# Attention over a window with an MLP over tokens behind it, in one kernel: tail evictions freed of the other bank of a PSUM pair, and the order written anew

## The chip, the cores and the metric

The kernel runs on one core of a Trainium2 chip. The metric is the time of the program on the device in microseconds (us). TensorE is called PE (its loads of weights PEld), VectorE DVE, ScalarE ACT, GpSimd POOL and SyncE SP.

## The reference

```python
# q, k, v: (8 batches, 8 heads, 576 positions, 64), float32
scores = (q @ k.T) / 8
bias = slopes[h] * -abs(i - j)                 # slopes 2**-(h+1)
mask = (i - j >= 0) & (i - j < 128)
attn = softmax(where(mask, scores + bias, -1e9))
x = (attn @ v) put together over heads         # (8, 576, 512)
wq, wk = x @ w_q, x @ w_k                      # (8, 576, 64) each
W_tok = wq @ wk.T / 8                          # (8, 576, 576)
out = maximum(W_tok @ x, 0) @ w_out            # (8, 576, 512), float32
```

## The kernel before

A batch has four blocks of 128 positions and a tail of 64. The kernel takes the batches in turn, and two batches at a time in the MLP. Each step is an operation with a short name; the number behind it is the batch (for the MLP the first batch of the two), then a part. In order of the data:

- **Loads.** `LF` (first batch, by SP and ACT queues), `Lq`, `Lk`, `Lv`, `Lt` (tails of q and k) on POOL's queue, which also converts to 16 bits; `Lw` and `Lwo` load the weights on SP's queue, and wait for `wz`, a tiny memset on DVE.
- **Set-up.** `ident` (POOL) and `idh` (its 16-bit copy, DVE), `iota` and `mask` (POOL) with `wmc` (DVE) between them, `bias` (ACT, 8 exponentials of the distances), `ones` (DVE: in each of the four buffers of v a memset of the unused half of the tail and one of a column of ones, whose product gives the sums), `zeros`, `pads`, `warm`; `WM` are matmuls on nothing that keep PE busy.
- **Transposes of q and k** on PE: `TF`, `TJ` (first batch), `TQ`, `TK`, `TT` (tails), and their evictions from PSUM `EF`, `EJ`, `ETQ`, `ETK`, `ETT`.
- **Attention.** `QK` b.g.u is the scores of block g and half u of the heads, `EXP` the exponential on ACT (L660), `MUL` the product with the bias on DVE (L669), `PV` b.t the product with v for query block t; t = 4 is the tail, which takes one bank instead of two. On DVE follow `RC`, the reciprocal of the sums (L723, for the tail L720 into `invt`), and `X`, the product that evicts (L733, for the tail L727 into `xtl`).
- **MLP.** `XT`, `XTT` transpose x, `EXT`, `EXTT` evict; `WQ`, `WK`, `WT` (tail) are the projections, `EWQ`, `EWK`, `EWT` their evictions; `G` is wk.T @ x and `EG` its eviction; `MX` the mixing, `RM`, `RMT` the relu that evicts it (`RM` one of the pair's two banks each); `OUT` the output product, `EO` its eviction, `DO` the store on SP's queue. `CWQ` and `CW` convert the weights.

PSUM is four tiles `pair0` to `pair3` of two banks each. Most products take a pair, the others one bank of a pair.

The order is written out by hand in the string `ORDER`: a word such as `QK0.2.1:P2` or `RC0.4:D` names the operation and its place (D, A, G, S: the engine; P2: pair 2, both banks; P21: pair 2, bank 1). `follow` reads it and each engine runs its operations in that order. Waits between engines come from the tiles that are read and written. As a pair is one tile, two operations in its two banks would wait for each other; `apart` declares such instructions free of order. It takes the instructions that an operation has handed to `hold`, puts them into a group of their bank and engine, and frees them of the other bank's groups of the other engines, other than true dependencies (`keep`). An operation finds its bank by its own PSUM (`banks`) or by what it frees (`frees`). `RC` and `X` hand nothing to `hold`.

The order of the first operations around the change is: on POOL `Lq0.2`, `iota`, `ident`, `Lk0.2`, `Lk0.1`, `Lk0.3`, `mask`, `Lq1.0`; on DVE `warm`, `ones`, `pads`, `idh`, `wmc`; on ACT `EF0.1.1`, `bias`, `EXP0.0.1`, `EXP0.2.1`, `EJ0.3.1`.

Of the kernel before, what the change touches and what calls it, by code (L numbers as in the profile page):

```python
# [45 lines left out]
warm:D LF0.0.1.1:A LF0.0.1.0:A LF0.0.0.1:S ones:D Lq0.2:G LF0.1.0.1:S LF0.1.0.0:S pads:D iota:G
LF0.0.0.0:S ident:G Lk0.2:G idh:D wmc:D Lk0.1:G WM.0:P31 TF0.0.1:P00 Lk0.3:G EF0.0.1:D
TF0.1.1:P01 mask:G EF0.1.1:A Lq1.0:G bias:A WM.1:P31 QK0.0.1:P0 TJ0.2.0:P10 Lt0:G TF0.1.0:P11
EJ0.2.0:D TJ0.2.1:P2 EF0.1.0:D Lk1.1:G zeros:D WM.2:P31 TJ0.1.1:P1 EJ0.2.1:D EXP0.0.1:A Lk1.0:G
EJ0.1.1:D QK0.2.1:P2 TF0.0.0:P30 Lk1.2:G EXP0.2.1:A MUL0.0.1:D TJ0.3.1:P0 QK0.1.1:P1 EF0.0.0:D  # L50
Lv0.0:G EJ0.3.1:A QK0.2.0:P2 MUL0.2.1:D EXP0.1.1:A Lk1.3:G EXP0.2.0:A MUL0.1.1:D Lv0.1:G
WM.3:P31 TQ1.0:P10 QK0.1.0:P0 ETQ1.0:D Lv0.4:G QK0.0.0:P2 EXP0.1.0:A TQ1.1:P11 ETQ1.1:D TT0:P3
EXP0.0.0:A Lv0.2:G ETT0:D MUL0.2.0:D WM.4:P01 QK0.3.0:P1 Lv0.3:G QK0.3.1:P2 ETT1:D EXP0.3.1:A
MUL0.1.0:D WM.5:P01 TK1.0:P3 Lq2.0:G ETK1.0:D EXP0.3.0:A Lv1.0:G MUL0.0.0:D WM.6:P01 QK1.0.1:P3
QK1.1.0:P2 MUL0.3.1:D EXP1.0.1:A PV0.0:P1 Lk2.0:G MUL0.3.0:D TK1.1:P0 EXP1.1.0:A Lk2.1:G
QK1.1.1:P3 RC0.0:D X0.0:D EXP1.1.1:A Lv1.1:G QK1.0.0:P2 ETK1.1:D PV0.1:P1 MUL1.1.0:D EXP1.0.0:A
Lv1.2:G QK1.2.0:P0 PV0.2:P3 RC0.1:D MUL1.0.1:D Lv1.3:G EXP1.2.0:A QK1.3.1:P2 MUL1.1.1:D Lv1.4:G
X0.1:D EXP1.3.1:A PV0.3:P0 RC0.2:D QK1.2.1:P1 RC0.3:D PV0.4:P20 X0.3:D EXP1.2.1:A MUL1.0.0:D
TQ2.1:P21 Lk2.3:G X0.2:D TQ2.0:P10 ETQ2.1:A PV1.0:P0 RC0.4:D Lk2.2:G MUL1.2.0:D QK1.3.0:P3
RC1.0:D EXP1.3.0:A Lv2.1:G X1.0:D wz:D MUL1.3.1:D Lw:S WM.7:P11 TK2.0:P0 ETQ2.0:A Lv2.0:G  # L60
XT0.0:P21 X0.4:D PV1.1:P3 Lwo.3:S MUL1.2.1:D ETK2.0:A Lt1:G XT0.1:P20 Lwo.2:S RC1.1:D
MUL1.3.0:D PV1.2:P1 Lwo.0:S EXT0.0:A X1.1:D QK2.0.0:P0 Lwo.1:S Lq3.0:G EXT0.1:A RC1.2:D
PV1.4:P21 X1.2:D PV1.3:P3 Lk3.3:G RC1.4:D EXP2.0.0:A QK2.0.1:P1 X1.4:D XT1.0:P20 RC1.3:D
Lk3.2:G X1.3:D EXP2.0.1:A XTT0:P0 EXT1.0:D Lv2.2:G XT1.1:P21 EXTT0:D QK2.1.0:P1 CWQ:A TK2.1:P3
EXT1.1:D Lk3.1:G QK2.1.1:P0 EXP2.1.0:A WT0:P20 MUL2.0.1:D WK0:P21 ETK2.1:D EWT0:A Lk3.0:G
EXP2.1.1:A MUL2.0.0:D QK2.2.1:P3 EWK0:D WQ0:P20 EXP2.2.1:A CW.3:D G0:P21 MUL2.1.0:D EWQ0:A
MUL2.1.1:D CW.2:A Lv3.4:G QK2.2.0:P3 MUL2.2.1:D EG0:A PV2.0:P0 EXP2.2.0:A CW.1:D MX0.0:P2
RC2.0:D PV2.1:P1 X2.0:D RM0.0:A Lv2.4:G MX0.4:P3 RC2.1:D TT2:P0 RM1.0:A X2.1:D RMT0:A MX0.2:P2
CW.0:D MX0.1:P1 ETT2:A ETT3:D XT2.0:P30 RM0.2:D RM1.2:A QK2.3.1:P0 EXT2.0:D RM0.1:A MX0.3:P2
Lv2.3:G TQ3.1:P31 RM1.3:A RM0.3:D TQ3.0:P30 RM1.1:A Lq4.0:G ETQ3.1:D QK2.3.0:P2 EXP2.3.1:A  # L70
TK3.1:P1 MUL2.2.0:D Lv3.3:G OUT1.3:P31 ETK3.1:D EXP2.3.0:A Lk4.1:G PV2.2:P0 ETQ3.0:D EO1.3:A
QK3.3.1:P1 RC2.2:D Lk4.0:G QK3.2.1:P2 X2.2:D EXP3.3.1:A OUT0.2:P31 MUL2.3.1:D Lk4.2:G
EXP3.2.1:A QK3.3.0:P0 MUL3.3.1:D TK3.0:P1 Lv3.2:G OUT1.4:P30 ETK3.0:D EXP3.3.0:A Lk4.3:G
MUL2.3.0:D QK3.2.0:P1 EO0.2:A QK3.1.0:P2 MUL3.2.1:D PV2.3:P0 Lv3.1:G EXP3.1.0:A EO1.4:D
OUT1.1:P31 RC2.3:D EXP3.2.0:A MUL3.3.0:D PV2.4:P30 TQ4.1:P20 X2.3:D Lt2:G EO1.1:A TQ4.0:P21
RC2.4:D ETQ4.1:A PV3.4:P00 X2.4:D ETQ4.0:D QK3.0.0:P1 QK3.1.1:P3 EXP3.0.0:A Lv3.0:G OUT0.3:P01
RC3.4:D MUL3.2.0:D X3.4:D Lq5.0:G EXP3.1.1:A QK3.0.1:P2 MUL3.1.0:D TK4.0:P1 OUT0.0:P00 Lv4.4:G
ETK4.0:D EXP3.0.1:A MUL3.1.1:D Lk6.0:G XTT2:P1 QK4.1.0:P3 EO0.0:A MUL3.0.0:D PV3.3:P2
EXP4.1.0:A Lk5.1:G OUT0.1:P00 EXTT2:D RC3.3:D MUL3.0.1:D Lk5.0:G PV3.2:P3 EO0.1:A X3.3:D
WT2:P10 Lv5.0:G EO0.3:A RC3.2:D X3.2:D QK4.0.1:P2 EWT2:A TK4.1:P0 Lv4.0:G TT4:P3 EXP4.0.1:A  # L80
ETK4.1:D QK4.0.0:P1 ETT4:D Lk6.3:G PV3.1:P0 EXP4.0.0:A ETT5:D PV3.0:P2 MUL4.1.0:D QK4.2.0:P3
RC3.1:D XT2.1:P10 RC3.0:D EXP4.2.0:A X3.1:D OUT1.2:P11 X3.0:D EXT2.1:A MUL4.0.0:D Lk5.3:G
QK4.3.0:P3 QK4.2.1:P2 EXP4.3.0:A TQ5.0:P00 MUL4.0.1:D Lv4.1:G XT3.1:P10 ETQ5.0:D EO1.2:A
XT3.0:P01 Lk5.2:G EXT3.1:D EXP4.2.1:A TQ5.1:P00 EXT3.0:D Lv5.4:G QK4.1.1:P1 QK4.3.1:P3
MUL4.2.1:D TK5.0:P2 EXP4.1.1:A Lv4.3:G WK2:P01 ETK5.0:D EXP4.3.1:A Lv4.2:G ETQ5.1:D QK5.0.0:P2
QK5.1.0:P1 MUL4.1.1:D EXP5.0.0:A Lk6.2:G OUT1.0:P00 MUL4.3.1:D Lq6.0:G EWK2:A PV4.0:P3
MUL4.3.0:D QK5.0.1:P2 EXP5.1.0:A G2:P01 RC4.0:D Lk6.1:G X4.0:D EXP5.0.1:A MUL4.2.0:D Lv5.1:G
PV4.1:P3 MUL5.0.0:D EG2:A QK5.1.1:P1 Lv5.3:G TK5.1:P2 MUL5.1.0:D EO1.0:A WQ2:P01 EXP5.1.1:A
ETK5.1:D Lk7.0:G RC4.1:D MUL5.0.1:D QK5.2.0:P2 EWQ2:A Lk7.1:G PV4.3:P1 X4.1:D EXP5.2.0:A
TK6.1:P0 Lq7.0:G RC4.3:D MX2.3:P3 ETK6.1:D PV4.2:P2 RM3.3:A Lv6.1:G X4.3:D MX2.0:P0 RM2.3:A  # L90
RC4.2:D QK5.3.0:P1 RM3.0:A X4.2:D PV5.0:P3 EXP5.3.0:A TQ6.1:P01 RC5.0:D Lv6.0:G X5.0:D MX2.2:P2
RM2.0:A QK5.3.1:P1 MUL5.1.1:D MX2.1:P3 Lv5.2:G RM3.2:A TQ6.0:P00 ETQ6.1:D RM3.1:A PV4.4:P21
Lk7.2:G MUL5.2.0:D EXP5.3.1:A OUT3.2:P31 ETQ6.0:D Lt3:G RM2.1:A QK5.2.1:P1 MUL5.3.0:D TK6.0:P0
EO3.2:A XT4.0:P30 RC4.4:D ETK6.0:D EXP5.2.1:A OUT3.1:P31 Lv7.4:G MUL5.3.1:D RM2.2:A Lv6.2:G
X4.4:D TK7.0:P1 EO3.1:A QK6.0.0:P0 EXT4.0:D PV5.1:P2 EXP6.0.0:A ETK7.0:D QK6.1.1:P3 RC5.1:D
MUL5.2.1:D EXP6.1.1:A QK6.2.1:P1 Lk7.3:G TQ7.1:P00 X5.1:D TQ7.0:P01 EXP6.2.1:A Lv6.3:G ETQ7.1:D
QK6.1.0:P2 QK6.0.1:P3 ETQ7.0:D EXP6.1.0:A PV5.4:P00 Lv7.2:G MX2.4:P1 RC5.4:D OUT2.2:P01
MUL6.2.1:D EXP6.0.1:A Lv7.1:G MUL6.0.0:D PV5.2:P2 RMT2:A Lv6.4:G X5.4:D QK6.2.0:P3 RC5.2:D
XT4.1:P00 X5.2:D EXP6.2.0:A PV5.3:P1 MUL6.1.1:D XT5.0:P20 EO2.2:A Lv7.0:G RC5.3:D OUT2.3:P21
MUL6.1.0:D EXT4.1:A DO2.2:S Lv7.3:G X5.3:D QK7.0.1:P3 EO2.3:A TT6:P0 MUL6.2.0:D QK7.0.0:P1  # L100
EXP7.0.1:A DO2.3:S OUT3.0:P21 ETT7:D ETT6:D DO1.3:S EXT5.0:D EXP7.0.0:A DO0.3:S QK6.3.0:P3
TK7.1:P0 DO3.2:S XT5.1:P20 EXP6.3.0:A ETK7.1:D DO1.4:S QK7.1.0:P1 EXT5.1:D QK7.1.1:P0 DO0.2:S
EXP7.1.0:A PV6.2:P3 MUL7.0.0:D DO3.1:S WK4:P20 DO1.2:S EXP7.1.1:A RC6.2:D MUL6.0.1:D DO0.0:S
MUL7.0.1:D QK6.3.1:P1 EO3.0:A DO1.1:S PV6.1:P0 X6.2:D EXP6.3.1:A OUT2.0:P21 RC6.1:D X6.1:D
EWK4:A QK7.3.1:P1 MUL6.3.0:D QK7.3.0:P3 XTT4:P0 OUT3.3:P20 EXP7.3.0:A EXTT4:D MUL6.3.1:D
PV6.0:P0 MUL7.1.0:D EO3.3:A WT4:P30 EXP7.3.1:A PV6.4:P31 RC6.0:D X6.0:D WQ4:P20 EWT4:A
MUL7.3.1:D QK7.2.0:P1 EWQ4:A QK7.2.1:P0 RC6.4:D MUL7.3.0:D G4:P30 EXP7.2.1:A X6.4:D MUL7.1.1:D
EXP7.2.0:A PV7.4:P31 PV7.0:P0 EG4:D XT6.0:P20 EO2.0:A MUL7.2.0:D PV6.3:P1 EXT6.0:A OUT2.1:P21
RC7.4:D RC7.0:D X7.4:D RC6.3:D X7.0:D OUT3.4:P31 EO2.1:A X6.3:D DO2.1:S MX4.2:P2 EO3.4:A
MUL7.2.1:D XTT6:P0 DO2.0:S PV7.1:P1 RM4.2:A EXTT6:D DO0.1:S PV7.3:P3 RM5.2:A RC7.1:D X7.1:D  # L110
PV7.2:P0 MX4.1:P2 RC7.3:D RC7.2:D WT6:P10 X7.2:D RM4.1:A XT7.0:P11 RM5.1:A X7.3:D MX4.3:P0
MX4.0:P2 RM5.3:A XT6.1:P30 RM5.0:D XT7.1:P31 EWT6:D OUT5.3:P21 EXT7.1:A EXT7.0:D OUT5.2:P10
EXT6.1:D EO5.3:A RM4.3:A RM4.0:D OUT5.0:P31 DO5.3:S DO3.0:S WK6:P30 DO3.4:S EO5.0:D DO3.3:S
WQ6:P31 EWK6:A DO5.0:S DO1.0:S G6:P30 EWQ6:D OUT4.2:P31 EG6:A EO5.2:A MX6.4:P2 MX6.2:P0 DO5.2:S
MX6.3:P1 RMT6:A RM7.2:D OUT5.1:P30 RM7.3:A RM6.2:D EO4.2:A OUT4.3:P01 EO5.1:D RM6.3:A DO4.2:S
MX6.0:P2 DO5.1:S MX4.4:P3 MX6.1:P1 RM6.0:A RMT4:D OUT4.1:P00 EO4.3:A RM7.1:D OUT4.0:P20 DO4.3:S
EO4.1:A RM6.1:A OUT7.4:P11 DO4.1:S EO4.0:A RM7.0:A OUT5.4:P10 DO4.0:S EO7.4:A OUT6.1:P21
EO5.4:A DO7.4:S OUT6.2:P11 DO5.4:S EO6.1:A OUT6.3:P10 DO6.1:S EO6.2:A OUT6.0:P21 DO6.2:S
EO6.3:D OUT7.0:P11 DO6.3:S EO6.0:D OUT7.2:P10 DO6.0:S EO7.0:A OUT7.1:P21 DO7.0:S EO7.2:A
OUT7.3a:P11 DO7.2:S EO7.1:A OUT7.3b:P10 EO7.3a:A DO7.1:S EO7.3b:D DO7.3b:S DO7.3a:S  # L120
# [940 lines left out]
```

## Time and profile before

| | |
|---|---|
| time, median of 3 runs | 141.94 us (141.69 to 142.16) |
| the profiled execution's own time | 142.43 us |
| its span from first to last instruction | 140.7 us |
| mean granted clock of TensorE | 0.998 |
| matmuls | 2176, of which 24 on nothing (`WM`) |
| longest chain that ended last | PE 56%, ACT 13%, DVE 12%, DMA 10% of the span |

All durations below come from that one profiled execution. In a group of instructions, the numbers behind the bar are busy time in us and mean ns of one, then the idle time of the engine just before them, with what ended it. In a timeline a row has start, duration, engine, line, operation and tiles, and in brackets the idle time before it.

### The profile page before, as it was taken

What the parts mean: (1) busy time and instruction counts of PE and PEld (TensorE: products, weight loads), DVE (VectorE), ACT (ScalarE), POOL (GpSimd) and SP (SyncE); (2) the same over time, 40 slices, a digit from 0 to 9 for tenths busy, and PEclk for the clock granted to TensorE, in tenths of its full rate; (3) what the DMA queues carried; (4) which work ended last, traced back from release to release, by engine and by line L of the source; (5) the groups of instructions that cost most, each with busy time, mean ns of one, the idle gap of its engine ahead of it and who ended that gap; (6) DMA issues with size and microseconds to landing.
All of it is one profiled execution on the core that took longest, in us unless ns stands there. A gap on an engine that the chain in (4) does not pass through costs nothing.

```text
span 140.7 us, 5111 instructions
## 1 busy us (share of the span) xinstructions
PE 125.5 (89%) x2176; PEld 79.1 (56%) x2176; DVE 111.0 (79%) x236; ACT 114.0 (81%) x165; POOL 76.3 (54%) x99
## 2 busy tenths in 40 slices
...
GB/s 103 204 165 170 157 155 185 155 156 192 312 191 158 169 169 155 168 174 158 153 164 173 171 172 158 157 146 283 316 215 9 132 96 169 278 224 221 214 391 150
DMA packets 96087, 25.63 MB, mean 182 GB/s; under 512 B 83136, under 2 KB 91072, under 8 KB 96064
## 3 DMA queue, kind: packets, MB, share of 16 engines
...
q8 instruction: 17, 0.28, 0.8%
q14 instruction: 6, 0.05, 0.1%
...
## 4 chain that ended last, share of the span: by engine, by line
PE 56%; ACT 13%; DVE 12%; DMA 10%; issue 5%; POOL 1%; ACTq 0%; SPq 0%; DVEq 0%
PE pair L243 47%; PE pair L246 9%; DMA osb<-in_moe_w_k_dram 5%; DMA natq<-in_q_dram 5%; ACT pt L660 5%; DVE qkT L257 4%; ACT rm L877 2%; ACT bias L352 2%; DVE pt L669 2%; ACT osb L255 1%; DVE x L733 1%; ACT qkT L255 1%; DVE xtl L727 1%; DVE vt L337 1%; POOL wm L321 1%
## 5 line engine op out<-in xcount | busy, mean ns | idle before, releaser
L660 ACT ACTIVATE pt<-pair 128x1024 f16<-128x1024 f32 x64 | 63.0, 1035 | 2.8 <-PE pair L243 2.0
L669 DVE TENSOR_TENSOR pt<-pt,bias 128x1024 f16<-128x1024 f16 x64 | 42.0, 677 | 1.3 <-ACT pt L660 1.2
L402 POOL DMA_DIRECT2D vt<-in_v_dram x40 | 34.1, 872 | 8.2 <-DMA natq<-in_q_dram 4.2
L243 PE MATMUL pair<-wout_sb,rm 128*128 128x512 f16 (+1 forms) x132 | 31.2, 373 | 0.7 <-DVE xtl L727 0.6
L384 POOL DMA_DIRECT2D natk<-in_k_dram x31 | 27.7, 907 | 3.2 <-DMA natq<-in_q_dram 2.0
L243 PE MATMUL pair<-qkT 64*128 64x256 f16 (+2 forms) x320 | 23.3, 252 | 2.5 <-ACT pt L660 0.9
L257 DVE COPY qkT<-pair 128x1024 f16<-128x1024 f16 (+1 forms) x34 | 20.2, 612 | 3.8 <-PE pair L246 3.0
L243 PE MATMUL pair<-vt,pt 128*128 128x65 f16 (+1 forms) x576 | 21.9, 194 | 1.3 <-ACT pt L660 0.5
L243 PEld LDWEIGHTS <-pt 128*128 128x128 f16 (+1 forms) x576 | 18.9, 100 | 7.0 <-issue 4.6
L255 ACT COPY osb<-pair 128x512 f32<-128x512 f32 (+1 forms) x31 | 18.1, 590 | 5.1 <-PE pair L243 5.0
L733 DVE TENSOR_TENSOR x<-pair,inv 128x512 f16<-128x512 f32 x32 | 21.7, 686 | 0.6
L243 PEld LDWEIGHTS <-rm 128*128 128x128 f16 x132 | 11.6, 97 | 12.7 <-issue 2.2
L243 PEld LDWEIGHTS <-qkT 64*128 64x128 f16 x320 | 10.7, 94 | 11.8 <-issue 7.1
L877 ACT ACTIVATE rm<-pair 128x512 f16<-128x512 f32 x25 | 14.3, 619 | 2.2 <-PE pair L243 2.1
L257 DVE COPY osb<-pair 128x512 f32<-128x512 f32 (+1 forms) x6 | 3.9, 644 | 8.4 <-ACT osb L255 7.8
L246 PE MATMUL pair<-identh,natq 128*64 128x128 f16 (+1 forms) x256 | 8.9, 218 | 1.0 <-DMA natq<-in_q_dram 1.0
L246 PE MATMUL pair<-identh,x 128*128 128x128 f16 x128 | 9.5, 220 | 0.2 <-DVE xtl L727 0.2
L243 PE MATMUL pair<-warm 128*128 128x512 f16 x24 | 8.3, 464 | 1.2 <-DVE warm L298 1.2
L246 PEld LDWEIGHTS <-natq 128*64 128x64 f16 (+1 forms) x256 | 7.2, 110 | 3.2 <-DMA natq<-in_q_dram 2.0
L246 PEld LDWEIGHTS <-x 128*128 128x128 f16 x128 | 7.4, 97 | 1.9 <-issue 1.0
L388 POOL DMA_DIRECT2D natq<-in_q_dram x8 | 7.1, 891 | 2.3 <-PE pair L246 1.2
L246 PE MATMUL pair<-identh,natk 64*128 64x64 f16 x248 | 6.5, 190 | 0.7 <-DVE osb L461 0.6
...
## 6 DMA issues: line engine op xcount, KB each, us to landing
...
```

Of the source, the lines that this page charges most:

```text
L243: hold(nc.tensor.matmul(*a, **k))
L246: hold(nc.tensor.transpose(*a))
L255: hold(nc.scalar.copy(out_ap, in_ap))
L257: hold(nc.vector.tensor_copy(out=out_ap, in_=in_ap))
L352: nc.scalar.activation(out=bias[hp // 2][:, e, hp % 2, :], in_=wm, func=AF.Exp, scale=-(2.0 ** (-(h + 1))))
L384: return lambda: nc.gpsimd.dma_start(out=natk(b, n), in_=k[b, :, P * n:P * n + P, :].transpose([1, 0, 2]))
L388: return lambda: nc.gpsimd.dma_start(out=natq_s[b % NQ][r0 // QR:P].rearrange("p h r d -> p h (r d)"), in_=q[b, :, r0:512, :].rearrange("h ...
L402: return lambda: nc.gpsimd.dma_start(out=vtv(b, t)[:n, :, 0:D], in_=v[b, :, P * t:P * t + n, :].transpose([1, 0, 2]))
L660: nc.scalar.activation(out=pt, in_=two(hold_.bank).rearrange("p e c -> p (e c)"), func=AF.Exp, scale=SCALE)
L669: nc.vector.tensor_tensor(out=pv, in0=pv, in1=bt, op=ALU.mult)
L733: nc.vector.tensor_tensor(out=x_s[b % NX][qt].rearrange("p (g h d) -> p g h d", g=2, h=4), in0=sums(p)[:, :, :, 0:64], in1=box["inv"].unsq ...
L877: hold(nc.scalar.activation(out=out_ap, in_=in_ap, func=AF.Relu, scale=WSCALE))
```

## The change

1. `RC` and `X` of the tail (part 4) hand their instructions to `hold`, and `RC` knows its bank by a new field `src`: `apart` now frees them of the other bank of their pair, too.
2. `ones` becomes four operations, one for each buffer of v, and loads and products of batch b wait for the one of their buffer alone.
3. `WARM` has 21 matmuls in seven groups instead of 24 in eight.
4. `ORDER` is written anew from first to last word: engines, banks and sequence of most operations differ. 86 loads and set-up steps on POOL, all stores, transposes and products are there as before; DVE has two `EXT`, three `RM`, three `EO`, one `EWT` and one `CW` more, and ACT two `EXTT`, two `ETT`, one `ETQ`, one `ETK`, one `EWQ` and one `RMT` more.

```diff
-WARM = (6, 2, 2, 5, 1, 1, 3, 4,)
+WARM = (7, 4, 2, 3, 2, 1, 2,)
...
-        self.eng = self.bank = None
+        self.eng = self.bank = self.src = None
...
-        src = op if op.banks else (op.frees[0] if op.frees else None)
+        src = op if op.banks else (op.frees[0] if op.frees else op.src)
...
-    def mk_ones(o):
-        for t in vt_s:
-            nc.vector.memset(t[64:128, 4], 0.0)
-            nc.vector.memset(t.rearrange("p t h w -> p (t h) w")[:, :, D:D + 1], 1.0)
+    def mk_ones(t):
+        nc.vector.memset(t[64:128, 4], 0.0)
+        nc.vector.memset(t.rearrange("p t h w -> p (t h) w")[:, :, D:D + 1], 1.0)
...
-    sets = add("ones", "", "", -58, DVE(3.0), [], mk_ones)
+    sets = [add("ones", "", i, -58 + 10 * i, DVE(0.65), [], lambda o, t=t: mk_ones(t)) for i, t in enumerate(vt_s)]
...
-                                    [*(pvd.get((b - NV, x)) for x in (t, min(t + 1, 4))), sets])
+                                    [*(pvd.get((b - NV, x)) for x in (t, min(t + 1, 4))),
+                                     sets[b] if b < NV else None])
...
-        p = add("PV", b, qt, want, pe(0.27 if qt in (0, 4) else 0.48), need + [sets],
+        p = add("PV", b, qt, want, pe(0.27 if qt in (0, 4) else 0.48), need + [sets[b] if b < NV else None],
...
-                nc.vector.reciprocal(out=box["inv"], in_=sums(p)[:, :, 64])
+                hold(nc.vector.reciprocal(out=box["inv"], in_=sums(p)[:, :, 64]))
...
-                nc.vector.tensor_tensor(
+                hold(nc.vector.tensor_tensor(
                     out=xtl_s[GI[b] % 2][:, SIDE[b], :].rearrange("p (h d) -> p h d", h=4),
                     in0=sums(p)[:, :, 0:64],
                     in1=box["inv"].unsqueeze(2).broadcast_to([P, 4, 64]),
-                    op=ALU.mult)
+                    op=ALU.mult))
...
         rcp = add("RC", b, qt, want + 0.5, DVE(0.2), [p], rc)
+        rcp.src = p
```

Of the new `ORDER`, the start, the stage of the weights and the last stretch (as written):

```
warm:D LF0.0.1.1:A LF0.0.1.0:A LF0.0.0.1:S pads:D Lq0.2:G LF0.0.0.0:S LF0.1.0.0:S iota:G
LF0.1.0.1:S Lk0.2:G Lk0.1:G ident:G Lq1.0:G idh:D WM.0:P31 TF0.0.1:P00 wmc:D mask:G TF0.0.0:P01
Lt0:G bias:A EF0.0.0:D ones.1:D WM.1:P31 TF0.1.1:P01 Lk0.3:G TJ0.2.0:P10 EF0.1.1:D EF0.0.1:D
Lk1.1:G EJ0.2.0:D WM.2:P31 TJ0.1.1:P0 TF0.1.0:P11 Lk1.0:G EJ0.1.1:A ones.3:D EF0.1.0:A ones.0:D
QK0.1.1:P0 Lk1.3:G EXP0.1.1:A QK0.1.0:P1 ones.2:D QK0.0.0:P2 QK0.0.1:P3 Lk1.2:G zeros:D
EXP0.0.1:A MUL0.1.1:D Lv0.4:G TQ1.1:P00 EXP0.0.0:A MUL0.0.1:D TJ0.2.1:P3 Lv0.0:G EJ0.2.1:D
EXP0.1.0:A ETQ1.1:D WM.3:P01 QK0.2.0:P3 TT0:P2 Lv0.1:G TQ1.0:P01 EXP0.2.0:A TJ0.3.1:P1 ETQ1.0:D
Lv0.2:G QK0.2.1:P3 EJ0.3.1:D EXP0.2.1:A ETT0:D Lv0.3:G MUL0.1.0:D WM.4:P00 QK0.3.0:P1 ETT1:D
...
XT1.0:P30 EXP2.1.0:A ETK2.1:D XTT0:P0 MUL2.0.1:D QK2.2.1:P2 CWQ:A QK2.0.0:P1 EXTT0:D XT1.1:P31
...
RC7.1:D X7.1:D XTT6:P0 DO5.3:S MX4.4:P1 XT6.1:P21 EXTT6:A XT7.0:P30 RMT4:A EXT6.1:D XT7.1:P31
EXT7.0:D OUT5.2:P10 EXT7.1:A OUT5.4:P30 WK6:P31 EO5.4:D DO5.4:S WT6:P30 EWK6:D DO3.0:S WQ6:P21
EWT6:A EO5.2:D EO5.0:A G6:P11 EWQ6:A DO5.0:S DO2.0:S OUT4.3:P10 EG6:A DO5.1:S DO5.2:S MX6.2:P2
MX6.4:P3 MX6.0:P0 RM6.2:A RM7.2:D OUT4.0:P11 RMT6:A RM6.0:D MX6.3:P2 EO4.0:A MX6.1:P3 RM6.3:D
OUT7.4:P00 RM6.1:A DO4.0:S EO4.3:D RM7.3:A OUT6.1:P30 EO7.4:A RM7.0:D DO4.3:S OUT6.2:P21
...
```

More of the change, by code (lines that the diff above doesn't have):

```diff
@@ L41 @@
 LAST = (7, 3)
-WARM = (6, 2, 2, 5, 1, 1, 3, 4,)
+WARM = (7, 4, 2, 3, 2, 1, 2,)
 ORDER = """
[L46 to L120, printed above, removed]
+warm:D LF0.0.1.1:A LF0.0.1.0:A LF0.0.0.1:S pads:D Lq0.2:G LF0.0.0.0:S LF0.1.0.0:S iota:G
+LF0.1.0.1:S Lk0.2:G Lk0.1:G ident:G Lq1.0:G idh:D WM.0:P31 TF0.0.1:P00 wmc:D mask:G TF0.0.0:P01
```

61 lines of the change are left out of this document (added).

## The prediction

> **What bounds the kernel now.** I read the page's first part, then busy time by stretch, the groups by form, the tile view of the tails, and the timeline where these pointed.
>
> ```profile
> PE 125.5 (89%) x2176; PEld 79.1 (56%) x2176; DVE 111.0 (79%) x236; ACT 114.0 (81%) x165; POOL 76.3 (54%) x99
> ```
>
> ```profile
> 0.00:20.00 20.00, 16.98 (x224) 8.93 (x225) 13.61 (x36) 13.97 (x21) 17.60 (x31) 1.00 1.75 159
> 20.00:40.00 20.00, 16.02 (x364) 12.02 (x363) 17.55 (x40) 16.96 (x22) 16.08 (x19) 1.00 1.96 199
> 40.00:60.00 20.00, 18.07 (x338) 10.98 (x335) 18.06 (x37) 18.84 (x28) 16.16 (x20) 1.00 2.16 166
> 60.00:100.00 40.00, 39.14 (x816) 27.06 (x816) 38.98 (x79) 38.59 (x54) 26.50 (x32) 1.00 2.03 179
> 100.00:115.00 15.00, 14.44 (x284) 9.78 (x283) 13.50 (x32) 12.42 (x21) 0.00 (x0) 1.00 0.45 149
> 115.00:130.00 15.00, 15.00 (x134) 7.47 (x132) 7.51 (x14) 10.11 (x20) 0.00 (x0) 1.00 0.57 209
> ```
>
> The columns are PE, PEld, DVE, ACT and POOL busy, granted clock, DMA. Up to 40 us PE has 7.0 us of idle time, spent on loads and on the chain PE, ACT, DVE. From 40 to 115 it idles for only 3.35 of 75 us, and ACT and DVE are nearly as full (1.4 and 1.0 us idle in 60 to 100). From 115 on PE alone is full. Three engines are near their limit at once, so the only idle time a better order can win back after 40 us is some 3 us, and what the tails of the queries take of it is the first question.
>
> ```profile
> L660 ACT ACTIVATE pt<-pair 128x1024 f16<-128x1024 f32 x64 | 63.0, 1035 | 2.8 <-PE pair L243 2.0 <-ACT wk L255 0.4
> L669 DVE TENSOR_TENSOR pt<-pt,bias 128x1024 f16<-128x1024 f16 x64 | 42.0, 677 | 1.3 <-ACT pt L660 1.2
> ...
> L733 DVE TENSOR_TENSOR x<-pair,inv 128x512 f16<-128x512 f32 x32 | 21.7, 686 | 0.6
> ...
> L255 ACT COPY osb<-pair 128x512 f32<-128x512 f32 x30 | 17.8, 597 | 5.1 <-PE pair L243 5.0
> ...
> L877 ACT ACTIVATE rm<-pair 128x512 f16<-128x512 f32 x25 | 14.3, 619 | 2.2 <-PE pair L243 2.1
> ...
> L727 DVE TENSOR_TENSOR xtl<-pair,invt 128x256 f16<-128x256 f32 x8 | 3.4, 424 | 1.5 <-PE pair L243 0.8 <-PE pair L246 0.4 <-ACT rm L877 0.2
> ...
> L720 DVE RECIPROCAL invt<-pair 128x4 f32<-128x4 f32 x8 | 1.4, 179 | 1.5 <-PE pair L243 0.9 <-ACT qkT L255 0.4 <-ACT osb L255 0.2
> ...
> L257 DVE CAST wk<-pair 128x512 f16<-128x512 f32 x1 | 0.7, 691 | 1.2 <-PE pair L243 1.2
> ```
>
> The 16 tail instructions (L720, L727) are busy for 4.8 us in all, and DVE stood idle for 3.0 us just before them. That is odd for work that reads a bank long finished; two places show why.
>
> ```profile
> 56.58 1.04 PE L243 MATMUL pair<-wout_sb,rm 128*128 128x512 f16 x4
> ...
> 57.65 0.18 DVE L720 RECIPROCAL invt<-pair 128x4 f32<-128x4 f32 x1 [0.86 <-PE pair L243]
> ...
> 58.80 1.02 PE L243 MATMUL pair<-wout_sb,rm 128*128 128x512 f16 x4 [0.63 <-DVE xtl L727]
> ...
> 106.36 0.41 PE L243 MATMUL pair<-xtl,wkt 128*64 128x256 f16 x4
> ...
> 106.81 0.42 DVE L727 TENSOR_TENSOR xtl<-pair,invt 128x256 f16<-128x256 f32 x1 [0.79 <-PE pair L243]
> ...
> 107.28 0.80 PE L243 MATMUL pair<-vt,pt 128*64 128x65 f16 x24 [0.52 <-DVE xtl L727]
> ```
>
> At 57.65 the reciprocal of batch 3's tail (PV3.4, pair 0 bank 0) starts when OUT0.3 in bank 1 has ended at 57.62, and OUT0.0 then waits for the product. At 106.81 X6.4 (pair 3 bank 1) starts when G4 in bank 0 ends, and PV7.4 waits. These are waits for the other bank of a pair, which no data needs.
>
> **The change part by part.**
>
> *Tails free of the other bank.* What PE pays now:
>
> ```profile
> who waited for it (us, times):
>   PE pair L243: 1.1, 2
> ...
>   PE pair L246: 0.2, 1
> ```
>
> The matmul rows give 1.1 + 0.2 = 1.3 us of PE idle time behind the product (the weight loads overlap them). In the built programs, 15 waits of a tail for the other bank of its pair, or of that bank for a tail, stand before the change, and none in the new order. If PE sets the pace this gives -1.3; if DVE does, up to its 3.0 us of idle time; if the next wait stands right behind, 0. I take -1.3, as PE is the engine that is full to the end. Below 0 it could cost only through the order, priced below.
>
> *Set-up of v in four parts, and a later ident.*
>
> ```profile
> 3.18 2.66 POOL L384 DMA_DIRECT2D natk<-in_k_dram  x3
> ...
> 4.51 0.70 DVE L333 CAST wm<-wint 128x384 f32<-128x384 int32 x1
> ...
> 5.28 0.37 ACT L255 CAST qkT<-pair 128x256 f16<-128x256 f32 x1 [2.12 <-PE pair L246]
> ...
> 5.83 0.97 POOL L321 TENSOR_SCALAR_AFFINE_SELECT wm<-wm 128x128 f32<-128x128 f32 x4
> ...
> 6.83 3.41 ACT L352 ACTIVATE bias<-wm 128x384 f16<-128x384 f32 x8 [1.18 <-POOL wm L321]
> ...
> 10.15 1.91 ACT L660 ACTIVATE pt<-pair 128x1024 f16<-128x1024 f32 x2
> ...
> 11.96 0.57 ACT L255 COPY qkT<-pair 128x512 f16<-128x512 f16 x1
> ...
> 12.11 0.40 PE L243 MATMUL pair<-qkT 64*128 64x256 f16 x4 [0.40 <-ACT pt L660]
> ...
> 14.63 1.94 ACT L660 ACTIVATE pt<-pair 128x1024 f16<-128x1024 f32 x2 [0.25 <-PE pair L243]
> ...
> 17.16 8.68 ACT L660 ACTIVATE pt<-pair 128x1024 f16<-128x1024 f32 x9 [0.60 <-PE pair L243]
> ```
>
> The memsets leave the front of DVE, but ident now stands behind two loads of 0.89 us each (2.66 / 3) on POOL, so idh and wmc can't start early: wmc would end at about 5.8 instead of 5.21, and the mask starts at 5.83 either way, since POOL has Lq1.0 to issue before it. The moved memsets fall where DVE has 6.4 us of idle time in the first 20. Cost 0, bounds -0.3 and +0.5: should the mask slip, bias and every exponential behind it on ACT slip with it.
>
> *The new order, start.* Bias ends at 10.24 as before. Now EJ0.1.1 (0.57) and EF0.1.0 (0.37) stand on ACT between bias and the first exponential, and that one's scores QK0.1.1 need EJ0.1.1: 10.24 + 0.57 + 0.40 of matmul = 11.2 instead of 10.15, so +1.05. Given back: EJ0.3.1 leaves ACT (-0.57), and the four scores now issued together cover the two idle times of 0.25 and 0.60 (-0.85). New: QK0.2.0 and QK0.2.1 follow each other in pair 3, so the second waits for the first's exponential, and ACT for the second: 0.40 + 0.05. Sum +0.1; I take 0, with bounds -1.0 and +1.5 (nothing given back).
>
> The pair shared by two scores in a row is what a rule speaks against: the Trainium skill, Perfetto Trace Analysis, Optimizing Tensor Performance, says that independent matmul groups should rotate through PSUM banks, so that one's eviction overlaps the next one's matmuls. The row at 12.11 agrees for PE (0.40 us for the same pattern in pair 2); there ACT had EJ0.3.1 (11.96) to do meanwhile, which it now lacks. By the rule this term alone would cost 0.45, as taken.
>
> *The new order, the weights and the middle.*
>
> ```profile
> 36.54 0.62 ACT L255 CAST wqk_sb<-osb 128x512 f16<-128x512 f32 x1 [2.10 <-DMA osb<-in_moe_w_k_dram]
> ...
> 39.96 1.03 PE L243 MATMUL pair<-x,wk 128*64 128x512 f16 x8
> ```
>
> wz on DVE releases the loads of the weights. Ahead of it stand one MUL and two X fewer, and one tail more (0.68 + 2 x 0.89 with its reciprocal - 0.6, some 1.8 us less), against the later start of 1.05: the weights land within 1 us of 36.5, as now. EWK0 moves from DVE to ACT, behind exponentials: DVE's idle 1.2 us (wk row above) go, but G0 (39.96 now) then waits for EWK0 up to 0.6 us. ACT has one exponential more (1.0) done before CWQ, which pays for that. 0, bounds -1.0 and +1.0. The loads on POOL keep kind, number and nearly their order; each waits for the eighth before it, as now. Three warm matmuls fewer lie in waits: 0.
>
> *The new order, the end.*
>
> ```profile
> 118.11 1.10 PE L243 MATMUL pair<-wqk_sb,xT 128*128 128x64 f16 x32
> ...
> 124.67 0.72 PE L243 MATMUL pair<-wqT,gs 64*128 64x512 f16 x12
> ...
> 128.78 7.08 PE L243 MATMUL pair<-wout_sb,rm 128*128 128x512 f16 x36
> ```
>
> Four output tiles move from behind G6 to ahead of WK6 (118.11 now). PE's work is the same, but fewer tiles cover the last chain G6, EG6, MX6, RM6, OUT6. OUT6.1 needs RM6.1, fourth on ACT behind RM6.2, RMT6 and EO4.0: some 4 x 0.6 = 2.4 us (0.619 and 0.597 less their overlap), while PE has from MX6.2's end OUT4.0 and OUT7.4 (0.88 each: 7.08 for seven whole tiles and two halves) and small mixes of 0.5 (three of them take 0.72 at 124.67), 2.2 us. That is 0.2 late, and RM7.1 on DVE makes OUT6.3 as late again: +0.4. Bounds 0 and +1.2 (two evictions uncovered).
>
> **Sum.** -1.3 + 0 + 0 + 0 + 0.4 = -0.9. The profiled execution took 142.43 us, of which 140.7 are its span; it becomes 141.5 with a span of 139.8. The median of the runs, 141.94, lies 0.49 below the profiled one; at it the forecast is 141.0.
>
> **The rivals.**
>
> *Slower: ACT starts late and never catches up (143.4).* If the 0.57 and 0.85 us don't come back, because the exponentials then wait for DVE instead (EJ0.2.1 and EJ0.3.1 stand there between products), the +1.05 and +0.45 stay, and ACT, 96% busy from 60 to 100, has no room to recover. The tails' waits were then slack, as PE waits for ACT: 141.94 + 1.5 = 143.4. Against it: 3.0 us of ACT idle time in 20 to 40. It decides at CWQ: if it ends over 1 us later than 37.16, this is the case.
>
> *No change that counts (141.9).* Freed of the tails, PE runs into DVE, which has 1.0 us of idle time in 60 to 100 and now carries three more RM and three more EO. The gain then shrinks to the 0.52 at 107 less the end's 0.4. For it: the order places two-bank products on the same pairs right behind the tails (PV7.0 and PV7.3 behind X7.4 and X6.4), so a wait of another name could stand there.
>
> *Much faster: DVE sets the pace (139.3).* Then its 3.0 us of idle time before the tails count in full, less 0.4: 141.94 - 2.6 = 139.3. For it: DVE is 97% busy in 60 to 100. Against: PE is as full, and stays so for 20 us when DVE is half idle (115 to 130).
>
> The Trainium skill, Perfetto Trace Analysis, Identifying the Most-Contended Engine, would put its weight here: it holds matmul busy time a bad measure and takes weight-load occupancy instead, which is 56% in this trace against 79 and 81 for DVE and ACT. The 9.9 of 10 at the end, with both others idle, speak against taking that for the whole kernel.
>
> **How the numbers follow.** Forecast 0.40 (own range 139.9 to 141.5), much faster 0.18, no change 0.14, slower 0.28. A measurement of this kernel tells about 0.3% (0.4 us) from no change. Faster 0.40 + 0.18 = 0.58, same 0.14, slower 0.28. The range reaches from just under the fast rival to the slow one, 139.1 to 143.4, and leaves out the outer parts of both.
>
> **What would show it.** Right: no idle time over 0.2 us before L720 and L727 that another bank ended; first exponential near 11.2; CWQ's end within 1 us of 37.2; PE idle in 40 to 115 near 2 us; idle times of 0.1 to 0.3 us between MX6 and OUT6.3. Wrong: a first exponential after 12, PE idle in 20 to 40 above 5 us, or a new idle time on PE over 1 us in all behind two-bank evictions of pairs.

## The result and the profile after

| | median, us | ratio to before, with its 95% interval |
|---|---|---|
| before | 141.81 (141.44 to 142.16) | 1 |
| after | 139.70 (139.16 to 141.81) | 0.985 (0.980 to 0.990) |
| after again, in another session; before there 142.52 | 139.41 (138.86 to 140.29) | 0.9785 (0.9745 to 0.9825) |

Medians are over all runs; ratios leave disturbed runs out, so that a ratio need not be the quotient of two medians. The kernel after is faster by 2.1 to 3.1 us. The forecast was 141.0; both medians lie inside the range, but just below the forecast's own stretch of it (139.9 to 141.5), nearest to the rival "much faster" (139.3). The profile shown here is that of the second row: that execution took 139.17 us, with a span of 137.4 and a granted clock of 0.998. First the page's busy times, then busy time by stretch (PE, PEld, DVE, ACT, POOL; clock; DMA).

```profile
PE 125.7 (92%) x2173; PEld 78.9 (57%) x2173; DVE 113.5 (83%) x240; ACT 112.9 (82%) x161; POOL 76.8 (56%) x99
```

```profile
0.00:20.00 20.00, 16.87 (x211) 9.25 (x213) 11.14 (x32) 12.85 (x19) 18.07 (x31) 1.00 1.74 160
20.00:40.00 20.00, 16.58 (x396) 12.73 (x387) 19.39 (x45) 18.45 (x22) 15.11 (x18) 1.00 1.95 198
40.00:60.00 20.00, 19.21 (x360) 11.75 (x359) 19.75 (x40) 19.88 (x30) 15.55 (x19) 1.00 2.14 159
60.00:100.00 40.00, 39.82 (x803) 26.26 (x800) 38.97 (x80) 38.97 (x54) 28.07 (x34) 1.00 2.05 186
100.00:115.00 15.00, 14.83 (x238) 9.15 (x235) 14.43 (x31) 11.84 (x20) 0.00 (x0) 1.00 0.53 182
115.00:130.00 15.00, 15.00 (x172) 7.94 (x171) 8.68 (x15) 8.78 (x18) 0.00 (x0) 1.00 0.62 212
```

From 40 to 115 us PE now idles for 1.14 of 75 us (0.79 + 0.18 + 0.17) where it idled for 3.35. The first 20 us are emptier than before on DVE and ACT (11.14 against 13.61, 12.85 against 13.97). From 115 on nothing has changed: PE alone is full. The rows of the tails, in the groups by form:

```profile
L727 DVE TENSOR_TENSOR xtl<-pair,invt 128x256 f16<-128x256 f32 x8 | 3.3, 420 | 0.1
L720 DVE RECIPROCAL invt<-pair 128x4 f32<-128x4 f32 x8 | 1.4, 176 | 0.0
```

The work is the same, but the idle time of DVE before it is 0.1 us in all where it was 3.0; the other bank's products and evictions no longer end it.

### The profile page after: what moved, and what is told of

Same layout as the page of the kernel before. It is cut to its first block, busy times and chain, and to the rows that moved or that the text cites. A ratio compares the mean times of both kernels' runs of the same rounds, so it can differ in the third digit from the quotient of the medians.

```text
span 140.0 us, 5117 instructions
## 1 busy us (share of the span) xinstructions
PE 125.1 (89%) x2173; PEld 77.4 (55%) x2173; DVE 113.0 (81%) x240; ACT 112.9 (81%) x161; POOL 76.6 (55%) x99
## 4 chain that ended last, share of the span: by engine, by line
PE 55%; DMA 19%; ACT 12%; POOL 7%; issue 4%; DVE 0%; POOLq 0%; DVEq 0%
PE pair L243 46%; DMA natq<-in_q_dram 12%; PE pair L246 8%; DMA natt<-in_k_dram 7%; ACT pt L660 6%; POOL vt L401 3%; POOL natk L383 2%; ACT rm L878 2%; ACT osb L255 2%; ACT qkT L255 1%; POOL natq L387 1%; POOL natt L395 1%; ACT xTt L255 0%; ACT rmt L878 0%; DVE qkT L257 0%
## 5 line engine op out<-in xcount | busy, mean ns | idle before, releaser
L255 ACT COPY osb<-pair 128x512 f32<-128x512 f32 (+1 forms) x28 | 16.4, 598 | 5.9 <-PE pair L243 5.7
L257 DVE COPY qkT<-pair 128x1024 f16<-128x1024 f16 (+1 forms) x30 | 17.9, 618 | 2.5 <-PE pair L246 2.4
L878 ACT ACTIVATE rm<-pair 128x512 f16<-128x512 f32 x22 | 12.1, 620 | 0.9 <-PE pair L243 0.9
L255 ACT COPY qkT<-pair 128x1024 f16<-128x1024 f16 (+1 forms) x10 | 8.4, 866 | 2.6 <-DVE qkT L257 2.2
L257 DVE COPY osb<-pair 128x512 f32<-128x512 f32 (+1 forms) x9 | 5.9, 655 | 5.0 <-PE pair L243 3.6
L880 DVE TENSOR_SCALAR rm<-pair 128x512 f16<-128x512 f32 x10 | 6.7, 684 | 2.8 <-PE pair L243 2.8
L257 DVE COPY xT<-pair 128x1024 f16<-128x1024 f16 x12 | 7.9, 683 | 0.7 <-PE pair L246 0.7
```

Source lines behind the costliest of these rows:

```text
L255: hold(nc.scalar.copy(out_ap, in_ap))
L257: hold(nc.vector.tensor_copy(out=out_ap, in_=in_ap))
L878: hold(nc.scalar.activation(out=out_ap, in_=in_ap, func=AF.Relu, scale=WSCALE))
L880: hold(nc.vector.tensor_scalar(out=out_ap, in0=in_ap, scalar1=0.0, scalar2=WSCALE, op0=ALU.max, op1=ALU.mult))
```

## The experiments

"Old order" is the order of the kernel before, "new order" that of the kernel after. A difference of ratios of 0.01 is 1.4 us (the kernel before took 142.5 to 142.6 us in all three sessions of experiments).

### The two parts of the change, alone

The kernel after unchanged:

> The changed kernel once more, for a profile to compare stage by stage. All theories: 139.7 us beside 141.8, ratio 0.985. By the theory of the tails' waits PE's idle time in 40 to 115 us is about 1.3 us less than before, and the first 40 us are no shorter. By the rival of the order alone, the start to G0 (39.96 us before) comes a microsecond or more earlier. By the rival that DVE sets the pace, DVE's idle time before 104 us falls by 3 us and PE's falls less.

Measured: 139.41 us, 0.9785 (0.9745 to 0.9825). From 40 to 115 us PE's idle time fell by 2.2 us (3.35 to 1.14), not by 1.3, and DVE's by 2.6 (4.46 to 1.85). G0 came at 41.53 us, later than the 39.96 of before and not earlier, as the rival of the order alone had it. The order and the tails differ here together; the next two runs take them apart.

The declaration in the kernel before, old order:

```diff
-        self.eng = self.bank = None
+        self.eng = self.bank = self.src = None
...
-        src = op if op.banks else (op.frees[0] if op.frees else None)
+        src = op if op.banks else (op.frees[0] if op.frees else op.src)
...
-                nc.vector.reciprocal(out=box["inv"], in_=sums(p)[:, :, 64])
+                hold(nc.vector.reciprocal(out=box["inv"], in_=sums(p)[:, :, 64]))
...
-                nc.vector.tensor_tensor(
+                hold(nc.vector.tensor_tensor(
...
+        rcp.src = p
```

> The order of before, with the tails' reciprocal and product declared free of the other bank and nothing else changed. Tails' waits on PE's account: -1.3 us, 140.5 (ratio 0.991). DVE sets the pace: -2.5 to -3.0 us, 139.0 (0.980). Order alone: 141.8 (1.000), as the next wait stands right behind the one that goes.

Measured: 139.12 us, 0.977 (0.9733 to 0.9807). Five edited lines and a new one, without the new order, bring all that the whole change brings. The two places that the prediction showed look so in this kernel's timeline:

```profile
54.94 0.61 PE L243 MATMUL pair<-qkT 64*128 64x256 f16 x8
55.48 0.17 DVE L720 RECIPROCAL invt<-pair 128x4 f32<-128x4 f32 x1
55.49 1.04 PE L243 MATMUL pair<-wout_sb,rm 128*128 128x512 f16 x4
...
56.15 0.42 DVE L727 TENSOR_TENSOR xtl<-pair,invt 128x256 f16<-128x256 f32 x1
...
57.02 0.82 PE L243 MATMUL pair<-wout_sb,rm 128*128 128x512 f16 x3
...
102.96 1.05 PE L243 MATMUL pair<-x,wk 128*64 128x512 f16 x8
103.52 0.42 DVE L727 TENSOR_TENSOR xtl<-pair,invt 128x256 f16<-128x256 f32 x1
...
104.07 0.78 PE L243 MATMUL pair<-vt,pt 128*64 128x65 f16 x24
```

The reciprocal at 55.48 now starts before OUT0.3 (55.49) instead of behind it, and X6.4 at 103.52 runs beside G4 (102.96 to 104.01). OUT0.0 (57.02) and PV7.4 (104.07) start without the idle times of 0.63 and 0.52 us that stood before them.

The kernel after without the declaration (new order, both `hold` of the tail taken out, so that its tails are tied to the other bank again):

> The new order without the declaration: the tails wait for the other bank again, at other places than before. Tails' waits: 1.3 us slower than the changed kernel or more, 141.0 to 141.5 (0.995). Order alone: 139.7 (0.985), no slower than the changed kernel.

Measured: 141.6 us, 0.9896 (0.9862 to 0.993). The execution that was profiled took 143.2 us, with a granted clock of 0.83 from 20 to 40 us and of 1.00 from 40 to 130. In its groups by form the idle time of DVE before the tails is back:

```profile
L727 DVE TENSOR_TENSOR xtl<-pair,invt 128x256 f16<-128x256 f32 x8 | 3.3, 422 | 1.7 <-PE pair L243 0.7 <-ACT xT L255 0.6 <-PE pair L246 0.4
L720 DVE RECIPROCAL invt<-pair 128x4 f32<-128x4 f32 x8 | 1.4, 179 | 1.3 <-PE pair L246 1.0 <-PE pair L243 0.3
```

Of these 3.0 us, 1.56 stand before 30 us. From 40 us on DVE waits before three of the tails' instructions:

```profile
58.00 0.42 DVE L727 TENSOR_TENSOR xtl<-pair,invt 128x256 f16<-128x256 f32 x1 [0.35 <-PE pair L246]
...
93.32 0.18 DVE L720 RECIPROCAL invt<-pair 128x4 f32<-128x4 f32 x1 [0.27 <-PE pair L243]
...
94.80 0.42 DVE L727 TENSOR_TENSOR xtl<-pair,invt 128x256 f16<-128x256 f32 x1 [0.72 <-PE pair L243]
```

That is 1.34 us. By stretch, from the first matmul of G0 to that of G4, first with free tails (the kernel after), then with tied ones:

```profile
41.53:101.87 60.34, 59.51 (x1201) 39.08 (x1201) 59.03 (x120) 59.05 (x83) 43.11 (x51) 1.00 2.06 183
44.11:105.96 61.85, 59.77 (x1202) 39.21 (x1202) 59.16 (x120) 59.35 (x83) 41.07 (x48) 1.00 1.98 184
```

The stretch is 1.51 us longer with tied tails.

So the declaration is worth 0.023 (3.3 us) in the old order and 0.011 (1.6 us) in the new one; the new order is worth 0.010 (1.5 us) with tied tails, and nothing that shows (+0.0015, inside both intervals) with free ones. The two do not add. Part of that has a place: the tied tails hold up DVE from 40 us on for 1.34 us in the new order and for 1.99 in the old one (next section). The rest was not found.

### Which tails

Old order, the declaration for some batches only:

```diff
+        free = hold if b >= 3 else (lambda i: None)    # the other kernel: b < 3
...
-                hold(nc.vector.reciprocal(out=box["inv"], in_=sums(p)[:, :, 64]))
+                free(nc.vector.reciprocal(out=box["inv"], in_=sums(p)[:, :, 64]))
...
-                hold(nc.vector.tensor_tensor(
+                free(nc.vector.tensor_tensor(
...
-        rcp.src = p
+        rcp.src = p if b >= 3 else None
```

> The kernel before with its old order; only the tails of batches 3 to 7 are declared free of the other bank. The tails freed in all eight batches gave a ratio of 0.977 (3.3 us). Theory S (the gain is the stalls of the tails from 57 us on, where PE, ACT and DVE are full): the sums of the shifts at RC3.4 to X6.4 are some 2.2 us, so the ratio is 0.983 to 0.986 if the 1.0 us at the weights needs the early tails, and 0.977 if that 1.0 us was no work of the tails. Theory M (the weights come earlier because the tails of batches 0 to 2 no longer stall DVE): 0.985 here. PE's account (1.3 us of idle time on PE): 0.991.

Measured: 140.45 us, 0.9851 (0.9803 to 0.99). This fits theory S as well as theory M.

> The kernel before with its old order; only the tails of batches 0 to 2 are declared free of the other bank. DVE stood idle for 0.43 + 0.44 + 0.17 us before them. Theory M (a stall of DVE in the first 40 us is passed on to the weights and the rest): 0.993, 1.0 us. Theory S (up to 40 us every engine has idle time, so that nothing is passed on): 1.000, within 0.3%.

Measured: 141.86 us, 0.997 (0.9929 to 1.001). Theory S's 1.000 lies inside the interval, theory M's 0.993 at its edge.

The five late tails bring 2.1 us, the three early ones 0.4 us, which the measurement can't tell from none. Together that is 2.5 of the 3.3 us; the remaining 0.7 is about the width of the intervals. These two kernels differ in nothing but the tails, so the same stretch can be laid side by side: from the first matmul of MX0.0 to that of PV7.4, first with the late tails free, then with them tied, and each followed by the tails in the groups by form, which count the whole kernel.

```profile
41.32:104.37 63.05, 61.53 (x1249) 40.76 (x1250) 61.00 (x125) 61.05 (x87) 42.31 (x50) 1.00 2.00 184
```

```profile
L728 DVE TENSOR_TENSOR xtl<-pair,invt 128x256 f16<-128x256 f32 x8 | 3.4, 421 | 0.5 <-PE pair L246 0.4
L721 DVE RECIPROCAL invt<-pair 128x4 f32<-128x4 f32 x8 | 1.4, 178 | 0.6 <-ACT qkT L255 0.5 <-ACT osb L255 0.2
```

```profile
41.28:106.38 65.10, 61.96 (x1248) 41.34 (x1249) 61.18 (x125) 62.16 (x88) 42.41 (x50) 1.00 1.96 179
```

```profile
L728 DVE TENSOR_TENSOR xtl<-pair,invt 128x256 f16<-128x256 f32 x8 | 3.4, 423 | 1.1 <-PE pair L243 0.8 <-ACT rm L879 0.2
L721 DVE RECIPROCAL invt<-pair 128x4 f32<-128x4 f32 x8 | 1.4, 176 | 1.0 <-PE pair L243 1.0
```

The stretch is 2.05 us longer with tied tails. DVE's idle time before them is 2.1 us (1.1 + 1.0), of which 1.99 stand in the stretch, at three places: 1.00 before RC3.4, 0.20 before X4.4 and 0.79 before X6.4. PE's idle time rises by 1.62 only (3.14 against 1.52); the other 0.43 stands in its row as busy time (61.96 against 61.53) for the same products. The kernel before and the one with all tails free differ alike in this stretch: 65.18 against 62.99 us, with 1.63 more idle time and 0.56 more busy time on PE. So the late tails' waits cost about as much as DVE's idle time before them, in both orders (2.05 for 1.99 here, 1.51 for 1.34 above), and PE's idle time shows it too low. Waits before 40 us were not seen to count in full: in the kernel before, DVE's idle time before the early tails was 1.04 us, 0.87 of it before 40 us, and freeing them brought the 0.4 us above, with an interval that reaches from none to 1.0.

### What sets the pace there

All tails free, old order; in the first kernel DVE has more work, in the second PE has.

```diff
# first kernel, behind the tail's product X
+                nc.vector.memset(scr, 0.0)             # 128x384 float32, read by nobody
# second kernel, in the tail's product PV
-                for h in range(4):
+                for h in (*range(4), *range(4)):
```

> The kernel before with its old order and all tails free (0.977), and behind each tail's product X DVE clears a tile of 128x384 that nobody reads, about 0.4 us, eight times. If DVE sets the pace from 57 to 110 us, the five of batches 3 to 7 cost in full: +2.0 us, ratio 0.991. If PE sets it and DVE only stood in its way: 0 to +0.5 us, 0.977 to 0.981.

Measured: 140.88 us, 0.9897 (0.9854 to 0.994), 0.013 or 1.8 us above the free tails alone. In number that is near the 0.991 of DVE setting the pace.

> The kernel before with its old order and all tails free (0.977), and the products PV of the tail are made twice, 0.44 us more on PE each, eight times; DVE's work is the same. If PE sets the pace from 57 to 110 us, the five of batches 3 to 7 cost in full: +2.2 us, ratio 0.992. If DVE sets it: 0 to +0.5 us, 0.977 to 0.981. If both are full, this and the run with more work on DVE each cost about 2 us.

Measured: 144.14 us, 1.011 (1.0061 to 1.016), 0.034 or 4.8 us above, which no theory had. The added work: of the first the group by form; of the second a doubled product in its timeline (PV6.4), and a single one (PV3.4) in that of the free tails alone; then the largest new gap in the second's timeline.

```profile
L733 DVE MEMSET scr<- 128x384 f32 x8 | 3.0, 378 | 0.2
```

```profile
105.71 0.68 PE L243 MATMUL pair<-vt,pt 128*64 128x65 f16 x32
```

```profile
54.59 0.42 PE L243 MATMUL pair<-vt,pt 128*64 128x65 f16 x16
```

```profile
64.74 0.80 PE L243 MATMUL pair<-vt,pt 128*128 128x65 f16 x21 [0.21 <-DVE qkT L257]
66.90 0.25 PE L243 MATMUL pair<-vt,pt 128*128 128x65 f16 x3 [1.36 <-issue]
```

The same stretch as above, from MX0.0 to PV7.4, in the free tails alone, with more work on DVE, and with more on PE:

```profile
41.08:104.07 62.99, 61.47 (x1249) 40.84 (x1251) 61.20 (x126) 61.01 (x87) 43.16 (x51) 1.00 2.02 186
42.02:105.94 63.92, 61.72 (x1249) 41.01 (x1250) 62.58 (x130) 61.37 (x87) 41.94 (x49) 1.00 1.98 181
42.75:108.83 66.08, 63.03 (x1329) 42.27 (x1330) 62.20 (x125) 61.78 (x88) 41.97 (x49) 1.00 1.89 174
```

Of DVE's eight memsets (3.0 us) four lie in this stretch, those of batches 2 to 5, 1.5 us in all. They make it 0.93 us longer. Ahead of it, MX0.0 starts 0.94 us later (42.02 against 41.08), but that is not the memsets' doing: wz, which stands on DVE before the first of them (30.61), is 0.92 us late already (29.59 against 28.67). So this profile gives 0.93 us as the price of the late memsets, and that the 1.8 us meet the expectation is in part luck.

PE's doubled product lasts 0.68 instead of 0.42 us, so that 2.1 us were added (8 times 0.26) and not the 3.5 of the expectation. Five of the eight, 1.3 us, lie in the stretch and make it 3.09 us longer: 1.36 us of that is one gap in which PE waited for nothing that the profile shows, and 1.73 is left. Another 1.67 us of the 4.8 stand ahead of the stretch (42.75 against 41.08). Part of them comes before any doubled product, as the second exponential waited until 11.54 us here and followed the first without a gap with free tails alone.

So neither theory stands alone: in this stretch added work on DVE costs about 0.6 of its length and added work on PE at least its length. These are single profiles, and a doubled product also delays the tail's reciprocal behind it on DVE, which was not separated. ACT, 38.6 of 40 us busy from 60 to 100 in the kernel before, was not given more work.

### Stages of the new order

All tails free; each kernel takes one order up to an operation and the other from there. The old order up to the eviction EG0 (43 us), then the new one:

> The order of before up to EG0 (42 us), then the new order; tails free, v set up in four parts one behind the other. Tails' waits: the start is worth nothing, so 139.7 (0.985), as the changed kernel. If the new start brings part of the gain: 140.3 or more. If the new start costs time, as in the rival of the late exponentials: 139.2 or less.

Measured: 141.08 us, 0.9895 (0.9865 to 0.9924).

The new order up to EG0, then the old one:

> All tails free; the new order (with the set-up of v in parts) until the first eviction of G, about 42 us, and the old order from there. Old order throughout gave 0.977, new throughout 0.9785, the old start before the new rest 0.9895. Theory N (the orders are worth the same in each stage, and the 0.9895 was the seam, where the old start hands over work that the new rest wants done otherwise): 0.976 to 0.982 here, if this seam is mild. Theory G (the new start gains some 1.5 us and the new rest loses as much): 0.967. Theory L (the start loses by its first exponential at 12.3 us instead of 10.2): 0.984.

Measured: 141.28 us, 0.9929 (0.9893 to 0.9964).

The old order up to PV7.3 (108 us), then the new one:

> All tails free; the old order until the product PV7.3, about 108 us, and the new order's end from there, with four output tiles ahead of the weights' product of batches 6 and 7 instead of behind it. The prediction's term for the end was +0.4 us with bounds 0 and +1.2: by it 0.980 (0.977 to 0.985). If the end costs nothing, 0.977; if it gains, as the time from 110 us on in the two profiles may suggest, 0.974.

Measured: 142.38 us, 0.9952 (0.9909 to 0.9995).

All three lose 1.6 to 2.6 us against either order throughout. The second lies outside all three theories named for it, and the third outside the prediction's bounds for the end. The first is slow as expected if the new start brought part of the gain, but then the second, which has that start, would be fast. The timelines of PE in the first and the third show the place, right at the seam:

```profile
43.14 0.62 PE L242 MATMUL pair<-qkT 64*128 64x192 f16 x16 [1.74 <-ACT qkT L254]
44.65 0.64 PE L242 MATMUL pair<-vt,pt 128*128 128x65 f16 x16 [0.89 <-ACT pt L659]
```

```profile
111.06 0.39 PE L242 MATMUL pair<-wqT,gs 64*128 64x512 f16 x2 [0.78 <-ACT rm L877]
112.32 3.63 PE L242 MATMUL pair<-wout_sb,rm 128*128 128x512 f16 x16 [0.86 <-DVE rm L879]
```

In the first PE stands still for 2.6 us (1.74 + 0.89), for an eviction and an exponential on ACT; in the third for 1.6 us, for the relu of mixes that the new order has done by then. In the second PE has no gap over 0.74 us from 33 to 50 us, and its loss is not placed. So the first and the third measure their seam, none of the three prices a stage, and none beats the kernel after. The version with the fewest edits, the old order with free tails, is as fast as the kernel after.

### The start's two terms

Two small edits in the kernel after. The set-up of v back in front:

```diff
-LF0.1.0.1:S ... EF0.0.0:D ones.1:D ... ones.3:D EF0.1.0:A ones.0:D ... ones.2:D
+LF0.0.0.1:S ones.0:D ones.1:D ones.2:D ones.3:D pads:D
```

> The kernel after, with the four parts of the set-up of v put back in front of the other work of DVE, as before. The prediction's term for moving them was 0 with bounds of -0.3 and +0.5 us. By it no change against the kernel after, 0.9785 (139.4 us). If the memsets in front held up the first transposes' evictions, +0.5 us, 0.982.

Measured: 139.34 us, 0.9808 (0.9753 to 0.9862).

The two evictions ahead of the first exponential on DVE:

```diff
-EJ0.1.1:A ones.3:D EF0.1.0:A
+EJ0.1.1:D ones.3:D EF0.1.0:D
```

> The kernel after, with the two evictions ahead of the first exponential on ACT (EJ0.1.1 and EF0.1.0) given to DVE, as before. The first exponential starts 0.9 us earlier, near 11.4. If the late start is given back before the weights, as the prediction took it (0), no change: 0.9785. If it is carried to the end: 0.972. If DVE, which then has 1.1 us more ahead of its first products, passes it on: 0.982.

Measured: 139.84 us, 0.9809 (0.9755 to 0.9863). ACT in the timeline of the kernel after (profile of the second row above), then of this one; then on PE, in the same two, WM.2 (two matmuls on nothing) and TJ0.1.1, the transpose that EJ0.1.1 evicts:

```profile
11.24 0.58 ACT L255 COPY qkT<-pair 128x512 f16<-128x512 f16 x1 [0.81 <-PE pair L246]
11.83 0.37 ACT L255 CAST qkT<-pair 128x256 f16<-128x256 f32 x1
12.32 2.85 ACT L660 ACTIVATE pt<-pair 128x1024 f16<-128x1024 f32 x3
...
17.49 6.57 ACT L660 ACTIVATE pt<-pair 128x1024 f16<-128x1024 f32 x7 [0.48 <-PE pair L243]
```

```profile
11.69 1.02 ACT L659 ACTIVATE pt<-pair 128x1024 f16<-128x1024 f32 x1 [1.25 <-PE pair L242]
```

```profile
10.15 0.83 PE L243 MATMUL pair<-warm 128*128 128x512 f16 x2
10.91 0.29 PE L246 MATMUL pair<-identh,natk 64*128 64x64 f16 x8
```

```profile
9.79 0.61 PE L242 MATMUL pair<-warm 128*128 128x512 f16 x2
10.33 0.29 PE L245 MATMUL pair<-identh,natk 64*128 64x64 f16 x8
```

Both intervals hold the kernel after's 0.9785: neither term shows in the time. They hold the 0.982 of the costlier theories as well, so that half a us would not have shown. And the second edit did not do what it was made for. The first exponential starts 0.63 us earlier (12.32 to 11.69), but TJ0.1.1 ends 0.58 us earlier, too (11.20 to 10.62), because the same transposes and matmuls ahead of it on PE took less time in that execution (0.72 and 0.61 us instead of 1.06 and 0.83). The run of the new start before the old rest shows the same without this edit: TJ0.1.1 at 10.33, the first exponential at 11.74. So the path to the first exponential goes through TJ0.1.1, its eviction on either engine and QK0.1.1; the edit moved it by about 0.05 us, and whether a late start is carried to the end was not tested by it.

## Why the prediction was right, and where it was off

**Direction and start.** Faster was the likelier side, and the reason was the right one: the tails' waits for the other bank are gone, and with them the time. The terms set at 0 (set-up, start, weights) held as a sum, as the new order shows no cost beside the old one with free tails; one by one they were not measured closer than half a us. The first exponential came at 12.32, not 11.2, and past the mark of 12 that the prediction had called a sign of being wrong. The step that missed it is the start's sum: it had EJ0.1.1 run right behind the bias, but EJ0.1.1 waited 0.81 us for its transpose TJ0.1.1, which stands on PE behind two matmuls on nothing (10.15 to 10.98). CWQ ended at 37.53, against 37.2 forecast. Its own decision point, a CWQ more than 1 us late, thus spoke rightly against the slower rival. How much of the lateness was given back by then can't be read from it: in kernels that keep the old order up to there, CWQ ended anywhere from 36.14 to 37.50. G0 was 1.57 us later than before (41.53 against 39.96), where the prediction had allowed 0.6; the time does not show it.

The shared pair 3 cost ACT 0.48 us (the row at 17.49) for 0.45 forecast. The Trainium skill, Perfetto Trace Analysis, Optimizing Tensor Performance, has independent matmul groups rotate through PSUM banks so that one's eviction overlaps the next one's matmuls. The row at 17.49 agrees.

**The term that was mis-sized.** "The tails' waits: -1.3" measured -3.3 us in the old order (-2.1 for the late five) and -1.6 in the new one. The prediction took PE's idle rows for the price and DVE's 3.0 us as a bound, "as PE is the engine that is full to the end". Two things were wrong in that. The 1.3 us are only what PE waited for a tail's product directly; its whole idle time in the stretch from MX0.0 to PV7.4 rose by 1.62 us for the late tails. And that idle time is itself too low a price: the late tails cost 2.05 us, and the rest stood inside PE's busy time. That PE is full to the end is true and settles nothing here, because DVE had little room either: 1.5 us of added work on it cost 0.93 in this stretch. The rival that counted DVE's idle time gave 139.3 and was right in number, but partly by luck. It took all 3.0 us, while in the new order the declaration brought 1.6 us, near the 1.34 of the late tails, and the other 1.5 us came with the order, which the rival priced as a loss of 0.4. Its name, "DVE sets the pace", says too much as well, since added work on PE cost more than its own length. One reason given against it, that both others are idle at the end, was misread: from 115 to 130 us, with PE busy for 15.00 of 15 us, DVE was busy for 7.51 and ACT for 10.11.

The Trainium skill, Perfetto Trace Analysis, Identifying the Most-Contended Engine, says to improve the engine with the highest occupancy first. By the busy shares that the prediction quoted beside it (81 for ACT, 79 for DVE) that would be ACT and not DVE. No run here shows a single such engine between 40 and 110 us: added work on DVE and on PE came out in part or in full, and ACT was not tried.

**The new order.** Its terms summed to +0.4, all of it at the end of the span, and with free tails it measured nothing. The times can't tell 0.4 us from nothing, but the rows of the end can. There PE has no idle time in the kernel after:

```profile
125.46 1.04 PE L243 MATMUL pair<-wout_sb,rmt 128*128 128x512 f16 x4
126.34 7.08 PE L243 MATMUL pair<-wout_sb,rm 128*128 128x512 f16 x36
```

The last nine output products follow without a gap, so the four tiles moved ahead of the weights' product were not missed as cover, and the waits of 0.1 to 0.3 us did not come. That the order is worth 1.5 us when the tails are tied, and nothing when they are free, no step of the prediction had: its sum added the two as if each had a price of its own. Shorter waits of the tied tails (1.34 against 1.99 us) are 0.65 us of that; the cause of the rest stays open.

**No change, slower.** Neither came. Of the wait that was to take the place of the tails', nothing is seen: PE's idle time in 40 to 115 is 1.14 us, under the 2 forecast.
